# Batch 0's squared norms by TensorE from the turned operands, omega by ScalarE's queue, ScalarE's table loaded first

## The chip, the cores and the metric

The kernel runs on one core of a Trainium2 chip. The metric is the device time of one execution in microseconds (us). The kernel before takes 980.41 us as the median of three runs (978.39 to 980.9). Engine names are those of the profile: PE is TensorE, DVE is VectorE, ACT is ScalarE, POOL is GpSimd, SP is the engine whose queue issues the transfers.

## The reference

A linear attention over random features, and behind it two feed-forward layers on 2304 rows of 512 columns. Cut to what matters here:

```
scale = 1 / sqrt(sqrt(64))                    # q, k: 4 batches, 8 heads, 576 rows, 64 columns
phi(x):  proj = x @ omega.T                   # omega: 128 features x 64
         h    = proj - sum(x*x) / 2           # the squared norm of each row
         return exp(h - max(h)) / sqrt(128)
kv  = phi(k*scale).T @ v;  z = sum of phi(k*scale) over rows
out = phi(q*scale) @ kv / (phi(q*scale) @ z + 1e-6)
x   = relu(out @ w_in)**2 @ w_out             # layer 1: 512 -> 2048 -> 512
xn  = x / rms(x) * rms_g
out = (silu(xn @ w_gate) * (xn @ w_val)) @ w_out2
```

All in float32. The kernel splits each operand of the large products into a high and a low part and adds three products.

## The kernel before, in words

The program has no loop at run time. A planner (class Plan, L43 to L244) is given every piece of work as a node with an engine, a planned duration, a priority and the buffers that it reads and writes; it plays the pieces through once when the program is built, and the order in which it starts them is the order in which they stand in each engine's queue. Each queue is worked off in that order on the chip: an instruction whose input is late holds up all behind it on its engine. Buffers come from classes with a fixed number of slots (L301 to L307): "t", "h" and "acc" are the eight PSUM banks (2, 2 and 4), "ld" (3) holds row-wise loads, "lt", "tt" and "tr" (2, 4, 1) the turned ones, "st" (3) the raw weights, "dw" (2) the decoded ones, "sm" (24) small statistics.

Where the planner finds TensorE idle before its time 45 us it puts in a filler: two products of a matrix of ones into a spare bank, L480, whose result nobody reads (L478 to L483, L221).

Attention (L519 to L752) runs per batch over four pairs of heads and over the "remainder", the last 64 rows of all heads. For each pair, k and then q is loaded twice: turned (64 columns of two heads on the 128 partitions, 512 rows along them; `operand`, L534) as TensorE's stationary operand, and row-wise (L563). From the row-wise copy `row_norms` (L527) takes the squared norms: a square by POOL, ACT or DVE, whichever the planner finds free (L498 to L500), and a sum over each row by DVE (L531). `features` (L568) multiplies the turned operand by omega (L577) into two banks, takes each row's maximum on DVE (L586), combines it with the norm in two small instructions (L590), and exponentiates on ACT (L598). Products with v (L637, L640), transposes (L691, L740) and the products of q with kv (L697) follow.

Layer 1 of batch j (`moe1`, L766) follows the attention of batch j, while the attention of batch j+1 is interleaved. In batch 0 each of the 32 weight units is loaded (raw, 512 KB), decoded by ACT and DVE (`decode`, L419: L430, L433 or L435, L439, L441, L444), and split into high and low by a cast on ACT (L401) and a subtraction on DVE or POOL (L392). L812 and L842 are the two products of layer 1.

Omega's 64 rows are loaded twice, to both halves of the partitions, by SP's queue (L485, through the helper `dma`, whose transfers all have line L386), and scaled by ACT (L489), which is ACT's first instruction and so the one in front of which its function table is loaded.

Of the kernel before, what the change touches and what calls it, by code (L numbers as in the profile page):

```python
# [9 lines left out]
F32 = mybir.dt.float32  # L10
# [4 lines left out]
AF = mybir.ActivationFunctionType  # L15
ALU = mybir.AluOpType
# [231 lines left out]
def kernel(  # L248
# [23 lines left out]
    nc = tc.nc  # L272
    PSUM = bass.MemoryType.PSUM
    B, SR, H, _ = rest_v.shape
    _, HP, P, _, R, D = q_r.shape
# [10 lines left out]
    SCALE = float(D) ** -0.25  # L286
# [4 lines left out]
    const = ctx.enter_context(tc.tile_pool(name="const", bufs=1))  # L291
# [16 lines left out]
    plan = Plan(slots)  # L308
# [38 lines left out]
    ones = const.tile([P, P], F32R, name="ones")  # L347
    om2 = const.tile([P, M], F32, name="om2")
    oms = const.tile([P, M], F32, name="oms")
    g_sb = const.tile([P, KC], F32, name="g_sb")  # L350
    eps_sb = const.tile([P, 1], F32, name="eps_sb")
    v_t = [att.tile([P, 2, R, D + 1], F32, name=f"v{i}") for i in range(2)]
    vr_t = att.tile([P, H * (D + 1) + 8], F32, name="vr")[:, :H * (D + 1)].rearrange("p (h n) -> p h n", h=H)
    kv_t = [att.tile([P, 2, 80], F32, name=f"kv{i}")[:, :, :D + 1] for i in range(2)]
# [4 lines left out]
    b_oms = Buf(ap=oms)  # L359
# [7 lines left out]
    def f32(t):  # L367
        return t.bitcast(F32)
# [5 lines left out]
    def dve(n):  # L374
        return 0.07 + n * 0.00104

    def pool(n):
        return 0.19 + n * 0.00216
# [4 lines left out]
    def dma(prio, outap, inap, nbytes, r=(), w=(), after=()):  # L383
        return plan.add(
            "SP", nbytes / 311e3, prio,
            lambda: nc.sync.dma_start(out=outap(), in_=inap()), r, w, after, tail=2.0,  # L386
        )
# [73 lines left out]
    T0 = -40.0  # L461
# [10 lines left out]
    b_late, b_eps = Buf(ap=ones), Buf(ap=eps_sb)  # L472
    plan.add("DVE", 0.3, T0, emit_ones, w=[b_late])
    plan.add("POOL", 1.0, T0, lambda: make_identity(nc, ident), w=[b_const])
    plan.add("POOL", 0.3, T0 + 2, emit_late, w=[b_eps])
    b_vz = Buf(ap=vr_t)
    plan.add("POOL", 0.6, T0 + 1, emit_zero_rows, w=[b_vz])
    def filler(bank):  # L478
# [2 lines left out]
                             rhs=ones.rearrange("p (o n) -> p o n", o=1).to_broadcast([P, 2, P]), start=True, stop=True)  # L481

    plan.filler = Buf(["acc"]), filler  # L483
    b_om = Buf(ap=om2)
    for h in range(2):  # L485
        dma(T0, lambda h=h: om2[h * D:(h + 1) * D, :], lambda: omega_t, 32768, w=[(b_om, h)])
    dma(T0 + 30, lambda: g_sb, lambda: rms_g.rearrange("(k p) -> p k", p=P), 2048, w=[b_g])

    plan.add("ACT", 0.4, T0, lambda: nc.scalar.activation(out=oms, in_=om2, func=AF.Copy, scale=SCALE), [b_om], [b_oms])  # L489

    def copy(prio, out, src, n, rd, wr):

# [3 lines left out]
    def square(prio, x, xa, n):  # L496
        opts = (
            ("POOL", pool(n), lambda: nc.gpsimd.tensor_tensor(out=xa(), in0=xa(), in1=xa(), op=ALU.mult)),  # L498
            ("ACT", act(n), lambda: nc.scalar.activation(out=xa(), in_=xa(), func=AF.Square)),  # L499
            ("DVE", Shared(dve(n)), lambda: nc.vector.tensor_tensor(out=xa(), in0=xa(), in1=xa(), op=ALU.mult)),  # L500
        )
        plan.add(*opts[0][:2], prio, opts[0][2], [x], [x], alts=opts[1:])
# [16 lines left out]
    def attention(b):  # L519
        base = (b - 1) * float(C1) if b else -25.0  # L520
        step = 3.7 if b else 6.0
        lead = base - (6.0 if b else 2.85)
        long = b >= LONG
        rem_x, rem_p = [], []
        ssr = Buf(["sm"])

        def row_norms(prio, x, ss):  # L527
            square(prio, x, lambda: x.ap, 512)
            plan.add(
                "DVE", dve(512), prio,  # L530
                lambda: nc.vector.tensor_reduce(out=ss.ap[:, :8], in_=x.ap, op=ALU.add, axis=AX), [x], [ss],  # L531
            )

        def operand(ldp, src, cls):  # L534

            x = Buf(["lt", cls])
            dma(ldp, lambda: x.ap, src, 262144, w=[x])
            return x

        def rem_prep(pr0):  # L540
            rem_x[:] = [operand(lead, lambda: rest_t[b].rearrange("p h n -> p (h n)"), "tr")]
            xr = Buf(["ld"], view=lambda t: t.rearrange("p h r d -> p (h r) d"))
            dma(lead, lambda: xr.ap, lambda: rest_r[b], 262144, w=[xr])
            row_norms(pr0, xr, ssr)
            dma(lead, lambda: vr_t[P - SR:], lambda: rest_v[b], 133120, w=[b_vr])

        def pair(hp):
            banks = ["t"] if b else ["t", "h", "acc"] if hp < 3 else ["t", "acc"]
# [6 lines left out]
            ld = pb - 3.0  # L555
            dma(ld + 0.1, lambda: vt, lambda: v_r[b, hp], 266240, w=[bv])
            stats = {}

            def transposed(nm, p0):
                ss = stats[nm] = Buf(["sm"])  # L560
                src, src_t = (k_r, k_t) if nm == "k" else (q_r, q_t)
                xs = operand(ld, lambda: src_t[b, hp], "tt")
                x = Buf(["ld"], view=lambda t: t.rearrange("p h r d -> p (h r) d"))  # L563
                dma(ld + 0.05, lambda: x.ap, lambda: src[b, hp].rearrange("p h r d -> p (h r) d"), 262144, w=[x])
                row_norms(p0, x, ss)
                return xs
# [38 lines left out]
            u = step / 10.0  # L605
            pk, pq = Buf(["p"]), Buf(["p"])
            xk = transposed("k", pb)
            features(pb + u, pk, xk, ODD, stats["k"], list(last_q))
            if hp == 0:
                rem_prep(pb + u)  # L610
                rem_p[:] = [Buf(["pr"])]
                features(pb + 2 * u, rem_p[0], rem_x[0], ODD, ssr)
            pr = rem_p[0]
            xq = transposed("q", pb + 2 * u)
            last_q[:] = [features(pb + 4 * u, pq, xq, ODD, stats["q"])]

# [76 lines left out]
            def mm(h):  # L693
                np, qt = nps[h], qts[h]
                for r in range(R):
                    for cs in HALVES:
                        nc.tensor.matmul(np.ap[cs, r * D1:(r + 1) * D1],  # L697
                                         lhsT=qt.ap[:, r * P + cs.start:r * P + cs.stop],
                                         rhs=kvt[:, h, :], start=True, stop=True)
                if h == 0:  # L700
                    for g in range(2):
                        nc.tensor.matmul(np.ap[:SR, (R + g) * D1:(R + g + 1) * D1], lhsT=qrt.ap[:, g, :],
                                         rhs=kvt[:, g, :], start=True, stop=True)
# [477 lines left out]


    attention(0)
    for b in range(B):
        if b + 1 < B:
            attention(b + 1)
        moe1(b)
# [104 lines left out]
```

## Time and profile before

| | |
|---|---|
| median of three runs | 980.41 us (978.39 to 980.9) |
| the profiled execution, its own time | 981.26 us |
| its span, first to last instruction | 979.1 us |
| PE busy | 960.5 us (98%), 5996 instructions |
| DVE busy | 690.7 us (71%) |
| ACT busy | 513.9 us (52%) |
| POOL busy | 73.8 us (8%) |
| bytes moved | 179.46 MB, mean 183 GB/s |

A view of windows gives, for each stretch in us from the span's start, the busy time of each engine with the number of its instructions in brackets, the granted TensorE clock as a share of full speed, the busy share of the 16 DMA engines, and GB/s. A timeline row is start, duration, engine, line, operation, output and input, count, and in square brackets the idle time before it and what ended that. "PEld" is the load of TensorE's stationary operand, "SPq" a transfer being issued by SP. In the timeline a float32 product shows as two entries where the program's order has one row. The chain of waits is the work that ended last, followed back; a row of it is start, length, what.

### The profile page before, as it was taken

The page shows a single profiled execution, that of the slowest core. Times are in us where ns is not written, and L with a number is a line of the kernel's source. Part 1 is how long each engine was busy: PE and PEld are TensorE (multiplying, and loading weights), DVE is VectorE, ACT ScalarE, POOL GpSimd, SP SyncE. Part 2 cuts the span into 40 slices and gives each one's busy share as a digit, 9 for nine tenths or more (in the row PEclk, how much of TensorE's full clock was granted, in tenths as well). Part 3 has the DMA queues.
Part 4 walks back from the last instruction along what each step waited for, and adds up shares of the span by engine and source line. Part 5 has one row for each costly group of instructions (what it writes and reads, how often), then busy time and mean ns, then how long its engine had stood idle before and what let it go on. Part 6 is the DMA issues. An engine that isn't in the chain of part 4 may idle for free.

```text
span 979.1 us, 16214 instructions
## 1 busy us (share of the span) xinstructions
PE 960.5 (98%) x5996; PEld 794.5 (81%) x5996; DVE 690.7 (71%) x1363; ACT 513.9 (52%) x1075; POOL 73.8 (8%) x70
## 2 busy tenths in 40 slices
PE   8999989999999999999999999999999999999998
PEld 8877767787788787887889988888887888888886
DVE  6898977677655665554554988989797747567673
ACT  6887776665545544544555657654353443314220
POOL 1123012010000000000000210000000000000000
PEclk9999999999999999999999999999999999999999
DMA  8878788888777765588879454234233221212203
GB/s 264 278 221 276 229 270 287 294 287 282 243 229 255 236 205 200 173 273 289 302 263 334 130 149 128 79 113 129 83 119 123 75 84 33 76 46 74 68 29 108
DMA packets 74846, 179.46 MB, mean 183 GB/s; under 512 B 8848, under 2 KB 12048, under 8 KB 74768
## 3 DMA queue, kind: packets, MB, share of 16 engines
q1 hardware_dynamic: 74768, 178.43, 56.2%
q8 instruction: 47, 0.77, 0.3%
q14 instruction: 31, 0.25, 0.1%
HBM read 143.27 MB, written 35.13 MB: 182 GB/s over the span
## 4 chain that ended last, share of the span: by engine, by line
PE 84%; DVE 7%; DMA 5%; ACT 3%; issue 1%; SPq 0%; POOL 0%; DVEq 0%; ACTq 0%; POOLq 0%
PE h L812 18%; PE acc L842 17%; PE acc L1054 11%; PE t L1115 11%; PE h L1054 10%; PE t L1054 4%; PE t L577 3%; PE t L697 2%; PE t L637 1%; DVE cc L1074 1%; PE t L691 1%; PE acc L480 1%; PE h L1115 1%; DVE oa L1123 1%; DMA st<-in_w_out_dram 1%
## 5 line engine op out<-in xcount | busy, mean ns | idle before, releaser
L842 PE MATMUL acc<-g,wr 128*128 128x512 f32 (+1 forms) x660 | 154.4, 378 | 3.7 <-POOL g L392 2.1
L842 PEld LDWEIGHTS acc<-g,wr 128*128 128x128 f32 x660 | 114.4, 191 | 27.3 <-POOL g L392 2.7
L812 PE MATMUL h<-x,wr 128*128 128x512 f32 x528 | 135.0, 398 | 0.5 <-ACT wr L401 0.5
L401 ACT CAST wq<-wq 128x512 fp32r<-128x512 f32 x108 | 66.0, 618 | 103.8 <-PE t L1115 16.6
L1115 PE MATMUL t<-wq,ub 128*128 128x512 f32 x474 | 116.6, 391 | 1.4 <-DVE oa L1123 1.3
L812 PEld LDWEIGHTS h<-x,wr 128*128 128x128 f32 x528 | 97.3, 189 | 22.1 <-ACT wr L401 0.7
L1054 PE MATMUL acc<-x,wq 128*128 128x512 f32 x324 | 107.0, 389 | 0.1
L1115 PEld LDWEIGHTS t<-wq,ub 128*128 128x128 f32 x474 | 88.5, 188 | 22.0 <-DVE oa L1123 2.9
L392 DVE TENSOR_TENSOR wq<-wq 128x512 fp32r<-128x512 f32 x108 | 80.1, 750 | 32.5 <-ACT wq L401 32.0
L826 ACT ACTIVATE f<-h 128x512 f32<-128x512 f32 (+1 forms) x80 | 44.8, 559 | 91.0 <-PE h L812 90.9
L1054 PE MATMUL h<-x,wq 128*128 128x512 f32 x252 | 85.3, 390 | 0.0
L392 DVE TENSOR_TENSOR g<-f,g 128x512 fp32r<-128x512 f32 (+1 forms) x64 | 43.3, 677 | 48.8 <-ACT f L499 36.8
L1054 PEld LDWEIGHTS acc<-x,wq 128*128 128x128 f32 x324 | 60.8, 188 | 13.2 <-DVE cc L1074 0.6
L598 ACT ACTIVATE p<-t,sm 128x128 f32<-128x128 f32 x224 | 62.2, 383 | 16.4 <-DVE sm L590 16.1
L1054 PE MATMUL acc<-xa,wq 128*128 128x512 f32 x192 | 69.9, 389 | 0.0
L842 PE MATMUL acc<-g,wu 128*128 128x512 f32 (+1 forms) x300 | 68.2, 373 | 0.0
L439 ACT ACTIVATE dw<-st 128x512 f32<-128x512 f32 x68 | 46.6, 688 | 41.0 <-DMA st<-in_w_out_dram 11.8
L1074 DVE TENSOR_TENSOR cc<-acc,cc 128x512 f32<-128x512 f32 x84 | 57.7, 687 | 12.9 <-PE acc L1054 11.7
L1123 DVE TENSOR_TENSOR oa<-t,oa 128x512 f32<-128x512 f32 x75 | 50.8, 686 | 21.8 <-PE t L1115 21.3
L812 PE MATMUL h<-x,wu 128*128 128x512 f32 x240 | 61.8, 402 | 3.0 <-ACT wu L401 3.0
L586 DVE TENSOR_REDUCE sm<-t 128x4 f32<-128x512 f32 x62 | 40.8, 684 | 28.3 <-PE t L577 26.7
L1054 PE MATMUL h<-xa,wq 128*128 128x512 f32 x168 | 60.5, 389 | 0.0
(232 smaller groups left out, 1647.9 us busy)
## 6 DMA issues: line engine op xcount, KB each, us to landing
wr<-w1d SPq DMA_DIRECT2D x88, 512.0 KB, 4.5
st<-in_w_out_dram SPq DMA_DIRECT2D x28, 512.0 KB, 4.7
w1d<-wr SPq DMA_DIRECT2D x22, 512.0 KB, 3.9
st<-in_w_in_dram SPq DMA_DIRECT2D x16, 512.0 KB, 4.6
st<-in_w_gate_dram SPq DMA_DIRECT2D x12, 512.0 KB, 6.0
st<-in_w_val_dram SPq DMA_DIRECT2D x12, 512.0 KB, 5.5
st<-y SPq DMA_DIRECT2D x23, 256.0 KB, 4.0
v<-in_v_r_dram SPq DMA_DIRECT2D x16, 260.0 KB, 3.5
```

What stands on the lines that cost most here:

```text
L392: return lambda: en.tensor_tensor(out=lo(), in0=src(), in1=f32(hi()), op=ALU.subtract)
L401: first = plan.add("ACT", act(n), prio, lambda: nc.scalar.copy(out=hi(), in_=src()), rd, [whi], after, pre=[blo] if blo is not bhi else [])
L439: lambda: nc.scalar.activation(out=out(), in_=hf(), func=AF.Abs, scale=65536.0), [(st, 1)], [w])
L586: nc.vector.tensor_reduce(out=mx.ap[:, :R], in_=fp.ap, op=ALU.max, axis=AX)
L598: nc.scalar.activation(out=pbuf.ap[:, j, :], in_=fp.ap[:, i, :], func=AF.Exp, bias=mx.ap[:, i:i + 1])
L812: nc.tensor.matmul(hb.ap[:, :n], lhsT=u.ap[:, wl, kk * P:(kk + 1) * P], rhs=xcols(j, xl, kk)(), start=(gi == 0 and ii == 0), stop=(gi == l ...
L826: lambda: nc.scalar.activation(out=rb.ap[:, :n], in_=hb.ap[:, :n], func=AF.Relu), [hb], [rb])
L842: nc.tensor.matmul(accs[e].ap[:, :n], lhsT=u.ap[:, w, es], rhs=x.ap[:, :n], start=(c == 0 and i == 0), stop=(c == C1 - 1 and i == 2))
L1054: nc.tensor.matmul(bank.ap[:, cols], lhsT=u.ap[:, wl, c0 + kk * P:c0 + (kk + 1) * P], rhs=x[kk][xl].ap[:, :cols.stop - cols.start], start= ...
L1074: lambda: nc.vector.tensor_tensor(out=out.ap, in0=bank.ap, in1=x.ap, op=ALU.add), [bank, x], [out])
L1115: nc.tensor.matmul(o.ap, lhsT=x[xl].ap[:, c0:c0 + P], rhs=us[f"o{i}"].ap[:, wl, :], start=i == n == 0, stop=i == 1 and n == 2)
L1123: lambda: nc.vector.tensor_tensor(out=oa.ap, in0=o.ap, in1=oa.ap, op=ALU.add), [o, oa], [oa])
```

## The change

Four things are altered. In batch 0 the row-wise loads of q, k and the remainder (nine transfers of 256 KB) are dropped with their row norms; in their place `turned_norms` squares the turned operand on POOL, and TensorE multiplies each of its four 128-column pieces by a 128 x 2 matrix of zeros and ones ("heads"), which sums the squares of each head. The norms then lie in a PSUM bank, where the two small DVE instructions read them. Omega's two transfers are issued by ACT's queue instead of SP's; omega is scaled by DVE instead of ACT; and ACT's first activation is an exponential of one element of the ones, so that its table is loaded there. Batches 1 to 3 keep the row-wise norms.

```diff
+    warm = const.tile([P, 1], F32, name="warm")
+    heads = const.tile([P, 2], F32, name="heads")
...
+    def emit_heads():
+        nc.gpsimd.memset(heads, 0.0)
+        for h in range(2):
+            nc.gpsimd.memset(heads[h * D:(h + 1) * D, h:h + 1], 1.0)
+
+    b_heads = Buf(ap=heads)
+    plan.add("POOL", 0.4, T0 + 0.5, emit_heads, w=[b_heads])
...
-    b_om = Buf(ap=om2)
-    for h in range(2):
-        dma(T0, lambda h=h: om2[h * D:(h + 1) * D, :], lambda: omega_t, 32768, w=[(b_om, h)])
+    b_om, b_warm = Buf(ap=om2), Buf(ap=warm)
+    plan.add("ACT", 0.1, T0, lambda: nc.scalar.dma_start(
+        out=om2[:D], in_=omega_t), w=[(b_om, 0)], tail=2.0)
+    plan.add("ACT", 0.6, T0 + 0.1, lambda: nc.scalar.dma_start(
+        out=om2[D:], in_=omega_t), w=[(b_om, 1)], tail=2.0)
+    plan.add("ACT", 1.4, T0 + 0.2, lambda: nc.scalar.activation(out=warm, in_=f32(ones[:, :1]), func=AF.Exp), [b_late], [b_warm])
...
-    plan.add("ACT", 0.4, T0, lambda: nc.scalar.activation(out=oms, in_=om2, func=AF.Copy, scale=SCALE), [b_om], [b_oms])
+    plan.add("DVE", 0.2, T0, lambda: nc.vector.tensor_scalar(out=oms, in0=om2, scalar1=SCALE, scalar2=None, op0=ALU.mult),
+             [b_om], [b_oms])
...
+        def turned_norms(p0, x, banks):
+            x2 = Buf(["ld"], view=lambda t: t.rearrange("p h r d -> p (h r d)"))
+            plan.add("POOL", pool(512), p0,
+                     lambda: nc.gpsimd.tensor_tensor(out=x2.ap, in0=x.ap, in1=x.ap, op=ALU.mult), [x], [x2])
+            ss = Buf(banks)
+
+            def mm():
+                for i in range(R):
+                    nc.tensor.matmul(ss.ap[:, 2 * i:2 * i + 2], lhsT=x2.ap[:, i * P:(i + 1) * P], rhs=heads,
+                                     start=True, stop=True)
+
+            plan.add("PE", 0.22 * R, p0, mm, [x2, b_heads], [ss])
+            return ss
+
...
         def rem_prep(pr0):
+            nonlocal ssr
             rem_x[:] = [operand(lead, lambda: rest_t[b].rearrange("p h n -> p (h n)"), "tr")]
-            xr = Buf(["ld"], view=lambda t: t.rearrange("p h r d -> p (h r) d"))
-            dma(lead, lambda: xr.ap, lambda: rest_r[b], 262144, w=[xr])
-            row_norms(pr0, xr, ssr)
+            if b:
+                xr = Buf(["ld"], view=lambda t: t.rearrange("p h r d -> p (h r) d"))
+                dma(lead, lambda: xr.ap, lambda: rest_r[b], 262144, w=[xr])
+                row_norms(pr0, xr, ssr)
+            else:
+                ssr = turned_norms(pr0, rem_x[0], ["t", "h", "acc"])
...
             def transposed(nm, p0):
-                ss = stats[nm] = Buf(["sm"])
                 src, src_t = (k_r, k_t) if nm == "k" else (q_r, q_t)
                 xs = operand(ld, lambda: src_t[b, hp], "tt")
+                if not b:
+                    stats[nm] = turned_norms(p0, xs, banks)
+                    return xs
+                ss = stats[nm] = Buf(["sm"])
```

The planner lays all queues out anew. TensorE at the program's start, before: "ones" are the fillers, "oms" the scaled omega, lt the turned k and then q of pair 0, tr the remainder, and after that lt the k of pair 1.

```order
L480 MATMUL acc_180<-ones 128x256 x12
L577 MATMUL t_211<-oms,lt_188 128x128
...
L577 MATMUL h_230<-oms,lt_193 128x128
...
L577 MATMUL acc_257<-oms,tr_223 128x128
...
L480 MATMUL acc_180<-ones 128x256 x4
L577 MATMUL t_289<-oms,lt_245 128x128
...
L480 MATMUL acc_180<-ones 128x256 x28
L577 MATMUL t_365<-oms,tt_249 128x128
```

TensorE at the same place now (the ld tiles hold the squares; lt_189 and lt_195 are k and q of pair 0, tt_232 is k of pair 1):

```order
L489 MATMUL acc_182<-ones 128x256 x14
L611 MATMUL t_221<-oms,lt_189 128x128
...
L555 MATMUL h_241<-heads,ld_216 128x2 x4
L555 MATMUL h_254<-heads,ld_239 128x2 x4
L611 MATMUL acc_265<-oms,tr_211 128x128
...
L555 MATMUL h_287<-heads,ld_234 128x2 x4
L489 MATMUL acc_182<-ones 128x256 x2
L611 MATMUL t_304<-oms,lt_195 128x128
...
L555 MATMUL t_319<-heads,ld_259 128x2 x4
L489 MATMUL acc_182<-ones 128x256 x8
L611 MATMUL h_354<-oms,tt_232 128x128
```

The remainder now comes ahead of pair 0's q, a norm of four products stands beside each operand (nine in all), and fillers fall from 90 to 36 in the whole program.

ScalarE at its start, before (p holds the exponentials of a pair, pr those of the remainder, and an L499 row is a square for a norm):

```order
L489 ACT_TABLE_LOAD
L489 ACTIVATE oms<-om_76 128x128
L499 ACTIVATE ld_200<-ld_200 128x512
L499 ACTIVATE ld_207<-ld_207 128x512
L598 ACTIVATE p_213<-t_211,sm_243 128x128 x4
L499 ACTIVATE ld_226<-ld_226 128x512
L598 ACTIVATE p_213<-t_212,sm_247 128x128 x4
L499 ACTIVATE ld_272<-ld_272 128x512
L499 ACTIVATE ld_276<-ld_276 128x512
L598 ACTIVATE pr_259<-acc_257,sm_300 128x128 x4
L598 ACTIVATE pr_259<-acc_258,sm_309 128x128 x4
L598 ACTIVATE p_232<-h_230,sm_274 128x128 x4
```

ScalarE at its start now (ld_276 is the remainder of batch 1, row-wise):

```order
L494 DMA om_76<-in_omega_t_dram 64x128
L496 DMA om_76<-in_omega_t_dram 64x128
L498 ACT_TABLE_LOAD
L498 ACTIVATE warm<-ones 128x1
L632 ACTIVATE p_223<-t_221,sm_246 128x128 x4
L632 ACTIVATE p_223<-t_222,sm_250 128x128 x4
L512 ACTIVATE ld_276<-ld_276 128x512
L632 ACTIVATE pr_267<-acc_265,sm_292 128x128 x4
L632 ACTIVATE pr_267<-acc_266,sm_294 128x128 x4
L441 ACTIVATE dw_368<-st_285 128x512
L632 ACTIVATE p_306<-t_304,sm_329 128x128 x4
L632 ACTIVATE p_306<-acc_305,sm_339 128x128 x4
```

Batch 0's squares are gone from ScalarE; one square of batch 1 stands in front of the remainder's exponentials, and the first step of decoding a weight (L441, which was L439) has moved up to just behind them.

## Rows read from the trace of the kernel before

**Rows 1.** Windows: busy PE, PEld, DVE, ACT, POOL (count); clock; DMA share; GB/s.

```profile
5.00:50.00 45.00, 44.56 (x612) 39.81 (x613) 38.18 (x126) 37.40 (x113) 5.16 (x5) 1.00 0.88 285
50.00:170.00 120.00, 113.09 (x811) 86.56 (x811) 102.43 (x236) 89.42 (x195) 25.43 (x19) 0.96 0.79 256
170.00:979.00 809.00, 799.92 (x4571) 665.53 (x4566) 549.94 (x1003) 385.66 (x767) 42.03 (x38) 1.00 0.52 167
```

**Rows 2.** Chain of waits, 0 to 80 us: start, length, what.

```profile
1.36 2.14 DMA om<-in_omega_t_dram
3.57 1.28 ACT L489
7.38 3.99 DMA lt<-in_k_t_dram
12.66 3.54 PE acc L480 x28
31.26 1.09 PE t L577 x16
```

**Rows 3.** What TensorE waited for, 50 to 170 us: total, times, longest.

```profile
PE h L812 <- ACT wu L401: 3.0, 1, 3.0
```

**Rows 4.** Windows of TensorE alone: busy PE (count), clock, DMA share, GB/s.

```profile
52.00:54.00 2.00, 0.84 (x10) 1.00 0.98 303
54.00:58.00 4.00, 4.00 (x20) 0.57 0.68 206
122.00:126.00 4.00, 0.99 (x5) 1.00 0.95 328
126.00:130.00 4.00, 4.00 (x13) 0.57 0.75 246
156.00:160.00 4.00, 2.47 (x21) 1.00 0.69 231
160.00:164.00 4.00, 4.00 (x44) 0.57 0.50 148
```

**Rows 5.** Timeline, 0 to 46 us, several engines.

```profile
0.73 1.21 SPq L386 DMA_DIRECT2D om<-in_omega_t_dram  x2
1.05 2.93 PE L480 MATMUL acc<-ones 128*128 128x256 f32 x12 [1.05 <-DVE ones L464]
...
5.23 2.08 PE L577 MATMUL t<-oms,lt 64*128 64x128 f32 x16 [1.25 <-ACT oms L489]
...
12.76 0.63 ACT L499 ACTIVATE ld<-ld 128x512 f32<-128x512 f32 x1 [0.80 <-DMA ld<-in_k_r_dram]
...
14.40 2.15 ACT L598 ACTIVATE pr<-acc,sm 128x128 f32<-128x128 f32 x8
...
41.19 0.59 ACT L401 CAST x<-t 128x512 fp32r<-128x512 f32 x1 [1.62 <-PE t L740]
41.67 2.18 ACT L598 ACTIVATE p<-acc,sm 128x128 f32<-128x128 f32 x8
```

**Rows 6.** Groups by line and form, TensorE, 5 to 48 us: the fillers.

```profile
L480 PE MATMUL acc<-ones 128*128 128x256 f32 x78 | 12.0, 294 | 0.0
```

**Rows 7.** Timeline of TensorE, 30 to 65 us: stationary operands of 128 and 64 columns.

```profile
32.83 0.60 PE L691 MATMUL h<-ident,p 128*128 128x128 f32 x4
...
41.08 0.69 PE L637 MATMUL t<-v,p 128*64 128x65 f32 x16
```

**Rows 8.** One line each: durations in ns (min/median/max), first and last start.

```profile
L531 DVE TENSOR_REDUCE sm<-ld x36: 654/679/689, 7.0 to 244.5; 128x8 f32<-128x512 f32 x36
L498 POOL TENSOR_TENSOR ld<-ld x10: 1038/1040/1287, 17.2 to 218.4; 128x512 f32<-128x512 f32 x10
L590 DVE SCALAR_TENSOR_TENSOR sm<-sm,sm x144: 123/155/1021, 8.8 to 400.0; 128x4 f32<-128x4 f32 x144
```

**Rows 9.** Timeline of POOL, 32 to 34.7 us.

```profile
32.63 2.04 POOL L498 TENSOR_TENSOR ld<-ld 128x512 f32<-128x512 f32 x2 [4.14 <-DMA ld<-in_k_r_dram]
```

**Rows 10.** Timeline of DVE beside it.

```profile
33.31 0.39 DVE L590 SCALAR_TENSOR_TENSOR sm<-sm,sm 128x4 f32<-128x4 f32 x1
```

## Prediction

> **What bounds the kernel now.** I read the windows first, then the chain of waits, TensorE's waits, and the timeline of the first 50 us. TensorE is busy 799.92 of the 809 us behind 170 us [rows 1]: whatever is won or lost before that goes through to the end almost whole, since the later work hangs on TensorE. Ahead of that lie two stages with different limits.
>
> From 5 to 50 us, batch 0's attention, TensorE counts as busy 44.56 of 45 us, but 78 of its products there are fillers [rows 1, 6]. In the chain of waits 28 of them last 3.54 us [rows 2], so one costs 0.126 us and the 78 some 9.8 us. DVE and ACT are busy 38.18 and 37.40 us there: TensorE, DVE and ACT all run close to full, and none can move far ahead alone.
>
> From 50 to 170 us, layer 1 of batch 0 with the attention of batch 1, TensorE is idle 120 - 113.09 = 6.9 us, while DVE and ACT (102.43 and 89.42 us) decode and split the weights [rows 1]. The idle time lies in three stalls, and behind each of them stand 4 us in which the granted clock is 0.57 [rows 4], that is mostly the lower level of 1.2 GHz; each of these costs 4 x 0.43 = 1.7 us more. Stage loss: 6.9 + 3 x 1.7 = 12.1 us. The longest stall is 3.0 us for a weight's cast on ACT [rows 3].
>
> **The change, part by part.** *Start.* Before, the chain is omega's transfer (2.14 us from the second issue at 1.36), the table load (1.28) and the scaling on ACT; the first product of omega stands at 5.23 [rows 2, 5]. Now the table load lies beside the transfer. If ACT issues omega at the same times and it lands as fast, it is there at 3.5, and DVE's scaling, not shown before, lies between one small DVE instruction (0.155 us) [rows 8] and the 1.28 us of the table load that it must stay below to save anything; I take 0.25, so 3.8. SP's queue loses the 1.21 us of omega's issues [rows 5], so the turned k is issued at 0.73 instead of 1.94 at the earliest; before it was there by 5.23, within 3.3 us of its issue, so now by 4.0. Both are covered: 14 fillers instead of 12 at 2.93 / 12 = 0.244 us run to 1.05 + 3.42 = 4.47. The start moves by -0.76 us. Were omega as slow from ACT as the 3.99 us of a large transfer [rows 2], it would be 5.6 instead: +0.4.
>
> At the same moment POOL squares k. While POOL worked from 32.63 to 34.67, a DVE instruction of 0.155 us begun at 33.31 took 0.39 and ended as POOL's first square did [rows 8 to 10]. So if POOL is first, the scaling ends near 3.5 + 1.04 + 0.25 = 4.8, and the start moves by -0.4.
>
> The Trainium skill says of this ("SBUF — State Buffer", Who interferes with whom) that DVE and GpSimd share a pair of ports which the first holds for its whole instruction, and that a tensor_scalar can need it. The trace's 0.39 beside 0.155 agrees; by the rule the nine squares moved to POOL also hold up DVE, though the two small DVE instructions now read the norm from PSUM and no longer two SBUF inputs, so by it they go free.
>
> *Fillers.* 22 behind the first block instead of 78: 56 x 0.126 = -7.1 us of TensorE.
>
> *Norms.* Nine times four products, two entries each. No row shows a product with two columns. By 64-column stationary operands (16 entries in 0.69, 0.043 each) a norm costs 0.34 us; by the 128-column transposes (4 in 0.60, 0.15 each) 1.2 [rows 7]; by omega's products, float32 in two entries (16 in 1.09, 0.068) [rows 2], 0.55. The last are nearest in kind; I take 9 x 0.55 = +4.9 us, between +3.1 and +10.8. So TensorE alone would be ahead by 0.76 + 7.1 - 4.9 = 3.0 us.
>
> *POOL and the banks.* Nine squares of 1.04 us [rows 8] lie on an engine busy 5.16 of 45 us. The first norm is ready at about 4.0 + 1.04, under the sixteen entries of k's features (4.47 to 6.55 at the 2.08 us of before). The remainder's norm waits for POOL's third square, about 7.2, some 0.1 us. Each norm holds one of the eight banks until its four small DVE instructions have run; I cost that at nothing, because fillers stand where TensorE would wait; where the cover is missing it is the slower rival below.
>
> *ACT.* It loses batch 0's squares and the scaling, but now one square of batch 1 stands ahead of the remainder's exponentials, and its row-wise load is the twelfth transfer of SP's queue. Before, the eleventh large load landed at 12.76 [rows 5]; with 1.25 us less in front and 0.25 MB more at 285 GB/s (0.9), the new one lands near 12.4, its square (0.63) ends at 13.0, and the remainder's exponentials start there instead of at 14.40: -1.4 us. From there to the last exponentials of batch 0 ACT's order has the same 64 exponentials, and two decode steps, two weight casts and two squares more, one copy of a turned tile fewer: +5 x 0.63 = +3.2. Before it took 14.40 to 43.85, 1.62 us of it in one wait for TensorE [rows 5]. Without that wait now 13.0 + 27.8 + 3.2 = 44.0. So batch 0's attention ends no earlier (+0.1), though TensorE alone could do 3.0; but ACT then is 3.2 us of later work ahead.
>
> *DVE and transfers.* Nine sums of 0.679 us [rows 8] and one square leave DVE, about 6.8 us; nine loads of 256 KB (2.36 MB, 8.3 us at 285 GB/s) leave the queue. Both were covered; they come back as weights that are decoded earlier.
>
> *Layer 1.* ACT's lead of 3.1 us (3.2 - 0.1) is a little above the longest of the three stalls. Bounds: all three go with their slow clock (-12.1), or none, or another as long as the worst appears (+4.7). Because every queue is laid out anew, I credit one stall only, the 3.0 us for a cast with its 1.7 us: -4.7.
>
> *Sum.* +0.1 - 4.7 = -4.6 us against the profiled execution's 981.26, 2.2 of which lie outside the span: 976.7. The median of the runs lies 0.85 below that execution, so 975.8.
>
> **The rivals.** *A, the forecast*, 975.8, its own range 972 to 978.5.
>
> *B, the transfers and norms were hidden anyway.* ACT's lead is eaten where DVE is busy 102 of 120 us, stalls of the same sum remain, and only the start's 0.76 us come through: 980.4 - 0.8 = 979.6. For it: the three engines are near full in both stages, and squares of batch 1 have moved to ACT. Against: 6.8 us really leave DVE.
>
> *C, TensorE is the bound throughout.* The 3.0 us come whole, and two stalls go: the longest (4.7) and one of 1.5 + 1.7: 980.4 - 3.0 - 7.9 = 969.5. For it: the chain of the first 50 us is nearly all TensorE. Against: the ACT count above.
>
> *D, slower: the fillers that went kept TensorE's clock up.* A norm that is quicker than it was planned leaves TensorE waiting in the attention of batch 0 where no filler stands, since the order is fixed. Each gap of 1.2 us or more has cost itself and 1.7 us of half clock [rows 4], 2.9 in all. It decides from two such gaps on: 5.8 - 0.8, and the stalls of layer 1 stay: 985.4. For it: 56 fillers fewer. Against: from 5 to 50 us before, 0.44 us idle in all.
>
> *E, the change doesn't do what it says at its head:* omega from ACT's queue lands late, and the start, at 5.6, is 1.2 us later than forecast; otherwise as A: 977.0.
>
> **How the numbers follow.** A 0.45, B 0.26, C 0.14, D 0.10, E 0.05. About 0.3%, 2.9 us, is what a measurement of this kernel can tell from no change: the bounds are 977.5 and 983.3. Faster: 0.8 of A (0.36), C (0.14), more than half of E (0.03), 0.53. Within: the rest of A (0.09) and E (0.02), B (0.26), 0.37. Slower: D, 0.10. The range reaches from C's end to between B and D, 970 to 982.
>
> **What would show it.** In the changed profile: the first omega product at 4.4 to 4.9; a norm's eight entries in 0.4 to 0.7 us; the last exponentials of batch 0 ending within a microsecond of 44.0, with two more weights decoded by then; TensorE idle from 50 to 170 us down from 6.9 to some 4 us, and one stretch of half clock fewer. I am wrong if norms cost 1 us or more, if the granted clock falls before 45 us, or if the stalls of layer 1 sum to 12 us again.

## The result, and the profile after

The changed kernel takes 986.5 us (median of 8 runs, 983.49 to 991.87) where the kernel before took 980.34 beside it: a ratio of 1.008, 95% interval 1.006 to 1.010. It is 6 to 8 us slower; forecast were 4.6 us less. The profiled execution after took 990.53 us with a span of 988.6, at the upper end of its runs, so its rows are read for what happened and where, and the sizes are taken from the medians.

The windows of before [rows 1], now:

```profile
5.00:50.00 45.00, 42.62 (x488) 38.78 (x488) 26.71 (x89) 27.29 (x85) 9.28 (x10) 0.77 0.64 202
50.00:170.00 120.00, 115.06 (x911) 89.64 (x908) 105.96 (x258) 93.66 (x215) 24.06 (x18) 0.97 0.77 251
170.00:988.00 818.00, 811.65 (x4607) 668.06 (x4606) 549.70 (x1008) 389.82 (x773) 41.61 (x38) 1.00 0.51 167
```

Two things are to be seen. In the first stage TensorE still counts as busy 42.62 of 45 us, but it got through 488 instructions in place of 612, at a mean granted clock of 0.77 in place of 1.00 (before, the clock's record begins only at 9.99 us, and sixteen entries of omega's products took 2.08 us at 5.23 [rows 5] against 1.09 later [rows 2], so its 1.00 hides a half-speed start); DVE and ACT, busy 38.18 and 37.40 us before, fell to 26.71 and 27.29, by more than the work taken off them: they wait for TensorE. And the last stage, which the change doesn't touch, is longer, with TensorE's idle time still small (6.4 us now, 9.1 before). 4.2 us of the 9 more are lateness brought in from ahead, as the course of the work below shows; the rest is lost in the stage itself.

The head of the program answers to [rows 5]; timeline, several engines:

```profile
0.74 0.55 ACTq L494 DMA_DIRECT2D om<-in_omega_t_dram  x1
1.32 0.61 ACTq L496 DMA_DIRECT2D om<-in_omega_t_dram  x1
1.96 1.28 ACT L498 ACT_TABLE_LOAD   x1 [1.96 <-issue]
3.74 2.04 POOL L550 TENSOR_TENSOR ld<-lt 128x512 f32<-128x512 f32 x2 [1.50 <-DMA lt<-in_k_t_dram]
4.98 0.88 DVE L501 TENSOR_SCALAR oms<-om 128x128 f32<-128x128 f32 x1 [3.98 <-DMA om<-in_omega_t_dram]
5.92 1.16 PE L611 MATMUL t<-oms,lt 64*128 64x128 f32 x16 [1.50 <-DVE oms L501]
7.01 1.26 PE L555 MATMUL h<-heads,ld 128*128 128x2 f32 x8
8.50 1.87 PE L555 MATMUL h<-heads,ld 128*128 128x2 f32 x8 [0.23 <-POOL ld L550]
```

The table load lies beside the transfer, as forecast. But omega lands 3.66 us behind its second issue (4.98 - 1.32), not 2.14 as from SP's queue [rows 2], and its scaling lasts until POOL's second square is done: 4.98 + 0.88 = 5.86, against 3.74 + 2.04 = 5.78. The Trainium skill states ("SBUF — State Buffer", Who interferes with whom) that the two share a pair of ports which one holds for its whole instruction; the trace agrees, with 0.88 us where the prediction took 0.25. With omega alone, where POOL runs nothing beside it, the same instruction takes 0.23:

```profile
4.58 0.23 DVE L493 TENSOR_SCALAR oms<-om 128x128 f32<-128x128 f32 x1 [3.58 <-DMA om<-in_omega_t_dram]
```

The first product of omega stands at 5.92, not at 4.47, and 0.69 later than before.

Below 45 us, the windows of TensorE alone (busy, count, granted clock, DMA share, GB/s):

```profile
5.00:10.00 5.00, 3.85 (x31) 0.77 0.99 322
10.00:15.00 5.00, 5.00 (x30) 0.50 0.84 255
15.00:20.00 5.00, 5.00 (x31) 0.50 0.50 138
20.00:25.00 5.00, 5.00 (x61) 0.52 0.36 148
```

From 7.70 to 24.76 us TensorE was granted 1.2 GHz, though between 7 and 25 us it was never idle for more than 0.23 us. What it did before the clock fell: 1.50 us of idle time up to 5.92, sixteen entries of omega, and a norm begun at 7.01. A norm's eight entries last 1.87 us at half speed; the first norm behind it shows what they last at 2.4 GHz:

```profile
25.10 1.05 PE L555 MATMUL acc<-heads,ld 128*128 128x2 f32 x8
```

The last exponentials of batch 0 end at 55.99 + 1.19 = 57.2, where 44.0 was forecast:

```profile
55.99 1.19 ACT L632 ACTIVATE p<-acc,sm 128x128 f32<-128x128 f32 x4
```

The places of the stalls of layer 1 [rows 4] are full, without idle time and with the clock at 2.4 GHz:

```profile
122.00:126.00 4.00, 4.00 (x29) 1.00 0.67 242
126.00:130.00 4.00, 4.00 (x44) 1.00 0.88 290
156.00:160.00 4.00, 4.00 (x35) 1.00 0.89 321
160.00:164.00 4.00, 4.00 (x45) 1.00 0.94 326
```

One more difference has no answer in the change's text: in layer 2, where both kernels issue the same products in the same kind of rows, twelve of them in a row last 2.96 us now and 2.88 before. Its rows stand at the experiment that explains it.

### The profile page after: what moved, and what is told of

Same layout as the page of the kernel before. It is cut to its first block, busy times and chain, and to the rows that moved or that the text cites. A ratio compares the mean times of both kernels' runs of the same rounds, so it can differ in the third digit from the quotient of the medians.

```text
span 988.6 us, 16233 instructions
## 1 busy us (share of the span) xinstructions
PE 972.7 (98%) x6014; PEld 799.6 (81%) x6014; DVE 682.5 (69%) x1354; ACT 512.3 (52%) x1072; POOL 77.7 (8%) x77
## 4 chain that ended last, share of the span: by engine, by line
PE 88%; DVE 5%; DMA 4%; ACT 1%; issue 1%; POOL 1%; SPq 0%; POOLq 0%; ACTq 0%; DVEq 0%
PE h L846 18%; PE acc L876 18%; PE acc L1088 13%; PE t L1149 12%; PE h L1088 11%; PE t L1088 3%; PE t L611 3%; PE h L1149 2%; PE t L731 1%; PE t L671 1%; DMA ld<-in_k_r_dram 1%; PE t L725 1%; DMA ld<-in_rest_r_dram 1%; DMA st<-in_w_in_dram 1%; DMA tr<-in_rest_t_dram 1%
## 5 line engine op out<-in xcount | busy, mean ns | idle before, releaser
L876 PE MATMUL acc<-g,wr 128*128 128x512 f32 (+1 forms) x660 | 151.8, 374 | 2.0 <-POOL g L394 1.2
L1149 PE MATMUL t<-wq,ub 128*128 128x512 f32 x474 | 119.6, 396 | 0.5 <-DVE oa L1157 0.3
L394 DVE TENSOR_TENSOR wq<-wq 128x512 fp32r<-128x512 f32 x108 | 79.1, 740 | 35.1 <-ACT wq L403 34.7
L394 DVE TENSOR_TENSOR g<-f,g 128x512 fp32r<-128x512 f32 (+1 forms) x67 | 46.2, 690 | 49.1 <-ACT f L512 39.1
L632 ACT ACTIVATE p<-t,sm 128x128 f32<-128x128 f32 x216 | 59.5, 381 | 27.6 <-DVE sm L624 27.6
L441 ACT ACTIVATE dw<-st 128x512 f32<-128x512 f32 x68 | 46.6, 686 | 39.2 <-DMA st<-in_w_out_dram 8.5
```

What stands on the lines that cost most here:

```text
L394: return lambda: en.tensor_tensor(out=lo(), in0=src(), in1=f32(hi()), op=ALU.subtract)
L441: lambda: nc.scalar.activation(out=out(), in_=hf(), func=AF.Abs, scale=65536.0), [(st, 1)], [w])
L632: nc.scalar.activation(out=pbuf.ap[:, j, :], in_=fp.ap[:, i, :], func=AF.Exp, bias=mx.ap[:, i:i + 1])
L876: nc.tensor.matmul(accs[e].ap[:, :n], lhsT=u.ap[:, w, es], rhs=x.ap[:, :n], start=(c == 0 and i == 0), stop=(c == C1 - 1 and i == 2))
L1149: nc.tensor.matmul(o.ap, lhsT=x[xl].ap[:, c0:c0 + P], rhs=us[f"o{i}"].ap[:, wl, :], start=i == n == 0, stop=i == 1 and n == 2)
```

## The experiments

Theories: **T1**, the clock: TensorE works at half speed over the norm products of two columns. **T2**, the head: omega late, its scaling held up. **T3**, batch 1's row-wise loads, on which ACT and POOL wait in order. Later came **T4** (the norm products are costly in themselves), **T5** against **T6** (where the tiles lie, against the new order or the chip, slows layer 2) and **T7** against **T8** (distance of two operands, against the place of one).

### Wider norm products, nothing else

```diff
-    heads = const.tile([P, 2], F32, name="heads")
+    heads = const.tile([P, P], F32, name="heads")
...
-  nc.tensor.matmul(ss.ap[:, 2 * i:2 * i + 2], lhsT=x2.ap[:, i * P:(i + 1) * P], rhs=heads,
+  nc.tensor.matmul(ss.ap[:, i * P:(i + 1) * P], lhsT=x2.ap[:, i * P:(i + 1) * P], rhs=heads,
...
```

> Order, buffers and queues are those of the changed kernel; only the moving operand of each of the 72 norm products of batch 0 is 128 columns wide in place of 2 (the other 126 columns are zeros, their sums are not read). T1 (TensorE runs nearly idle through the stretches of two-column products, its granted clock stands at half from 7.7 to 24.8 us, and batch 0's attention is done at half speed): the clock is at full for most of 5 to 25 us, batch 0's work is 6 to 9 us less late, the kernel ends at 977 to 981 us. T2 (omega's late landing and its 0.88 us scaling set the clock back) and T3 (batch 1's row-wise loads arrive late): nothing of theirs is changed, 986 us, or a little more for the wider products.

979.73 us (ratio 1.0018, 1.0007 to 1.003). The clock stays at full from 4.77 to 55.97 us. The same windows as above:

```profile
5.00:10.00 5.00, 4.35 (x48) 1.00 0.99 325
10.00:15.00 5.00, 5.00 (x54) 1.00 0.92 317
15.00:20.00 5.00, 4.85 (x82) 1.00 0.89 306
20.00:25.00 5.00, 5.00 (x99) 1.00 0.23 66
```

and a norm of 128 columns lasts 1.05 to 1.16 us, little longer than one of two at full clock (0.95 to 1.05):

```profile
10.06 1.16 PE L555 MATMUL h<-heads,ld 128*128 128x128 f32 x8
```

T1 holds, and T2 and T3, whose causes were left in place, fall as the main one. An idle stretch stands ahead of omega here too (1.23 us, beside 1.50) and the clock did not fall behind it. The width costs little: at full clock the products last nearly as long with 2, 32 and 128 columns (1.05, 1.08 and 1.16 us for eight entries).

### The two halves of the change apart

Omega by SP's queue and scaled on ACT in the changed order; the norms alone, planned anew; omega and the table alone, planned anew.

```diff
-    plan.add("ACT", 0.1, T0, lambda: nc.scalar.dma_start(
+    plan.add("ACT", 0.1, T0, lambda: nc.sync.dma_start(
...
```

> The changed kernel with omega loaded by SyncE's queue and scaled on ScalarE again; the norms stay on TensorE, the order of everything else stays. T2: the first omega product comes at about 5.2 us in place of 5.9, TensorE has no idle stretch before it, the clock stays at full after 7.7 us, and the time is 978 to 981 us. T1: the first omega product comes earlier too, but the clock still falls before 10 us and stays at half for 15 us or more; 985 to 987 us. T3: 985 to 987 us as well.

> The kernel before with one part of the change, planned anew: batch 0's norms by TensorE from turned operands; omega is loaded and scaled as before. T1: a half-speed stretch of 10 us or more before 30 us, 984 to 987 us. T2: no such stretch, 977 to 981 us. T3: 984 to 987 us, with the granted clock at full from 10 to 40 us and the loss at the waits for batch 1's loads.

> The kernel before with the other part of the change, planned anew: omega by ScalarE's queue and scaled on VectorE, the table loaded first; batch 0's norms stay row-wise with their loads, fillers and VectorE's sums. T1: omega's first product within 0.7 us of the kernel before's 5.23, no half-speed stretch of 10 us before 40 us, 979 to 982 us. T2: the first product near 5.9, the clock falls before 10 us, 984 us or more. T3: 979 to 982 us.

986.24, 985.43 and 977.83 us (1.0071, 1.0071, 0.9991; the last interval 0.9979 to 1.0003). Omega back on SP and off DVE brings its first product to 5.42 us, the clock stands at half from 8.26 to 25.33, and the time is that of the changed kernel: T2 is not the main loss. (It isn't a clean test of the gaps: a wait of 1.77 us for POOL's square opens at 7.57.) The norms alone run at half speed until 20.04 us. I read from this that the norms were the whole loss and omega worth nothing. That was wrong in size, for a reason that all these kernels share and that shows only behind 500 us.

### The kernel before again, and with thin fillers

```diff
-            nc.tensor.matmul(bank[:, :2 * P].rearrange("p (o n) -> p o n", o=2), lhsT=ones,
-                             rhs=ones.rearrange("p (o n) -> p o n", o=1).to_broadcast([P, 2, P]), start=True, stop=True)
+            nc.tensor.matmul(bank[:, :2], lhsT=ones, rhs=ones[:, :2], start=True, stop=True)
```

> The kernel before, unchanged, as a control on the chip that runs the others: 978 to 980 us. What is asked of its trace: whether the stalls of layer 1 (at 122 and 157 us in the first trace) and the full pace of the products after 550 us (0.227 us apart) belong to this kernel or to one run. If they belong to the kernel, both stand there again, and what the changed kernel wins back of its late start between 120 and 170 us is the missing stalls; if to the run, the stalls are elsewhere or gone and the products after 550 us are 0.231 to 0.233 us apart as in the traces of the other kernels of this study, and the tail of the changed kernel (5 us lost after 550) is no effect of the change.

> The kernel before with its own order and its row-wise norms; each of the 78 fillers moves 2 columns in place of 256. T1 (products that move few columns leave the clock at half): the granted clock stands at half for 10 us or more before 30 us, batch 0's attention is 5 to 12 us late, 982 to 986 us. The rival T4 (the norm products are costly in themselves, by their weight loads or their place in the chain from POOL's squares, and the clock follows from the gaps): nothing of that is in this kernel, the clock rises at about 9 us as before, 977 to 980 us.

The control took 978.96 us (1.0004), the thin fillers 985.2 (1.0062, 1.0039 to 1.0085). Without any norm product and in the order of before, the clock stood at half from 12.07 to 25.72 us, in the control from 12.26 to 15.67. The windows, control first:

```profile
10.00:15.00 5.00, 4.04 (x36) 0.73 0.91 291
15.00:20.00 5.00, 5.00 (x48) 0.93 0.63 153
20.00:25.00 5.00, 5.00 (x88) 1.00 0.91 291
```

```profile
10.00:15.00 5.00, 4.19 (x39) 0.71 0.96 309
15.00:20.00 5.00, 5.00 (x25) 0.50 0.80 228
20.00:25.00 5.00, 5.00 (x61) 0.50 0.23 88
```

TensorE is as busy in both, and in both idle time lies ahead of the fall or around it (1.23 and 0.72 us with thin fillers, 2.04 in the control), so the fall itself may be due to that; what the fillers decide is how soon the clock is back. So the fillers of before did a second work for the clock. T4 falls as the main cause. The control's trace also has the stalls of layer 1 again, some 2 us later, so they belong to the order of before; and its products of layer 2 keep their pace, as do those of the kernel with thin fillers, while those of the changed kernel and of every kernel that has its new tiles don't.

### 32 columns, and a first attempt at a better kernel

> The changed kernel with its order kept and 32 moving columns in each norm product, between the 2 of the change and the 128 that gave 979.73 us. T1: the loss shrinks with the columns moved; the half-speed stretch of 7.7 to 24.8 us is shorter but not gone, 981 to 985 us. T4 (width matters only when the product is as long as its weight load takes): the eight entries still take 0.95 us or more, the clock falls as with 2 columns, 986 us.

> A version that may beat both: norms by 128-column products, their cost in the order's table set to the 1.0 us per eight that they took (1.76 in the changed kernel), omega by SyncE's queue first in its order and scaled on VectorE, the table still loaded first. T1: full clock from about 5 us to 40 us, no stall of TensorE over 2 us before 40 us, 976 to 979 us, the kernel before or a little under it. If the rest of the loss is in the row-wise loads of batch 1 (T3), it stays at 979 to 981 us.

986.96 and 989.39 us: both off. With 32 columns the clock's record has no entry before 23.05 us, but a norm lasts 1.91 us as at half clock, and nothing is won over two columns. That is the time that T4 had for it, not T1's; but its layer 2 is slower too (0.2334 us from product to product, against 0.2321 in the changed kernel, some 2 us in all), so the run by itself doesn't tell the two apart. The second keeps its clock from 4.77 to 144.72 us as expected and is slower all the same: it is stalled elsewhere (TensorE 26.85 of 30 us busy from 140 to 170), and its layer 2 is slow, which neither T1 nor T3 has a place for.

### Where the tiles lie

The change puts two new tiles, warm and heads, into the pool "const". With their rounding they move everything behind them on that side of the memory by 64 bytes a partition: x, xb, ub and g, which are one operand of layer 2's products, from 41152 to 41216 and so on in the compiled program. The other operand, wq, lies in a pool of the other side and stays at 171968. Layer 1 takes both operands (x or g with wr or wu) from the moved side. The wide norms moved it by 544 bytes, omega alone by 32, 32 columns by 160.

```diff
     eps_sb = const.tile([P, 1], F32, name="eps_sb")
+    const.tile([P, 16], F32, name="pad")
```

> The kernel before, its order untouched, with one unused tile of 64 bytes a partition behind eps_sb, so that every tile that follows in the pools on that side (x, xb, ub, g, xq among them) lies 64 bytes higher, as the two new tiles of the change (warm and heads) put it; the tiles of the other side (wq, xa) stay. T5 (the products after 550 us, whose two operands lie on the two sides, run slower by where the tiles lie): 0.2267 us from product to product becomes 0.231 to 0.234 after 550 us, nothing before 500 us changes, and the time is 984 to 986 us, 5 to 7 us over the kernel before. Rival T6 (the new order itself, or the chip's state, slows the late products): 978 to 980 us and 0.2267 us as before.

> The changed kernel with an unused tile that makes the sum of the new tiles 2048 bytes a partition in place of 64. T5: the late products are 0.2267 us apart again, the half-speed stretch of 7.7 to 24.8 us stays, 979 to 982 us. T6: 986 us.

> Norm products of 128 columns (which gave 979.73 us) and the same filling up to 2048 bytes. T1 and T5 together: no half-speed stretch before 40 us, late products 0.2267 us apart, 972 to 975 us, faster than both kernels. T6: 979.7 us.

> Omega by ScalarE's queue alone, row-wise norms (which gave 977.83 us), filled up to 2048 bytes. T5: late products 0.2267 us apart, 971 to 974 us; the part of the change that concerns omega and the table is then worth 5 us or more, hidden until now by the late products. T6: 977.8 us.

Measured: the kernel before with 64 unused bytes 986.4 us (1.0075, 1.0053 to 1.0098); the changed kernel filled up to 2048 bytes 978.74 (1.0003, 0.999 to 1.0017); wide norms filled up 972.21 (0.9946, 0.9927 to 0.9966); omega alone filled up 970.44 (0.9924, 0.9906 to 0.9943). T5 holds in all four, and T6 falls. The same row of twelve products, of the control, of the changed kernel, of before with 64 bytes, and of the changed kernel filled up:

```profile
659.49 2.88 PE L1115 MATMUL t<-wq,ub 128*128 128x512 f32 x12
```

```profile
663.14 2.96 PE L1149 MATMUL t<-wq,ub 128*128 128x512 f32 x12
```

```profile
659.43 2.96 PE L1116 MATMUL t<-wq,ub 128*128 128x512 f32 x12
```

```profile
652.77 2.88 PE L1150 MATMUL t<-wq,ub 128*128 128x512 f32 x12
```

From start to start that is (2.88 - 0.389) / 11 = 0.2265 us and (2.96 - 0.394) / 11 = 0.2333. Over all some 1640 products of 512 columns of layer 2 the mean is 0.2270 in the control and 0.2321 in the changed kernel: 1640 x 0.0051 = 8.4 us, which is what 64 unused bytes cost in the medians (8.5; by the ratio 7.3). The granted clock is 1.00 in both. Layer 1's products of 512 columns follow each other every 0.2282 us in both, and it keeps its count in equal time: 350 to 420 us, control and changed kernel:

```profile
350.00:420.00 70.00, 70.00 (x556) 1.00 0.55 194
```

```profile
350.00:420.00 70.00, 70.00 (x556) 1.00 0.56 193
```

### Distance or place, and the period

```diff
-    edge.tile([P, 8], F32, name="edge")
+    edge.tile([P, 24], F32, name="edge")
```

> The kernel before with its unused edge tile 96 bytes in place of 32, which puts wq, xa and the attention's tiles 64 bytes lower and leaves x, xb, ub, g where they were. T7: the distance changes by 64 bytes, 0.231 to 0.234 us after 550 us, 984 to 987 us. T8 (the place of x, ub and g alone decides): 0.2267 us, 978 to 980 us.

> Both sides moved: wq and xa 64 bytes lower, x, xb, ub and g 448 bytes higher, so that their distance changes by 512 bytes. T7: 0.2267 us after 550 us, 978 to 980 us. T8: 0.231 to 0.234 us, 984 to 987 us.

> The kernel before with 512 unused bytes in place of 64. T7 (what counts is how far apart the two operands lie, modulo 512 bytes): 0.2267 us from product to product after 550 us, as in the kernel before. If a multiple of 2048 is needed: 0.231 to 0.234.

> The kernel before with 256 unused bytes. T7: 0.231 to 0.234 us after 550 us, some 6 us more in all. If 256 bytes were the period: 0.2267 us.

> The kernel before with 128 unused bytes, between the 64 that slow the late products and the 256 that do not. Period of 128 bytes: 0.2267 us from product to product after 550 us, 976 to 980 us. Period of 256 bytes: 0.231 to 0.234 us, 984 to 987 us.

One execution each: 987.44, 980.55, 977.72, 975.94 and 982.49 us. The pace of the same row tells more than these times; moved on the other side alone, and on both:

```profile
660.46 2.96 PE L1115 MATMUL t<-wq,ub 128*128 128x512 f32 x12
```

```profile
658.41 2.88 PE L1116 MATMUL t<-wq,ub 128*128 128x512 f32 x12
```

With 512 and 256 bytes it is 2.88, with 128 bytes 2.94; the last two:

```profile
654.61 2.88 PE L1116 MATMUL t<-wq,ub 128*128 128x512 f32 x12
```

```profile
655.49 2.94 PE L1116 MATMUL t<-wq,ub 128*128 128x512 f32 x12
```

T8 falls, since moving wq's side alone is enough and moving both undoes it. T7 holds, but not with the 512 bytes that it had named: 32, 64, 128, 160 and 544 bytes are slow, 256, 512 and 2048 are not, as a period of 256 bytes would have it. What counts is the distance between the two sides. One thing doesn't fit the distance between a product's own operands: products of xa and wq, which lie on one side and keep theirs, are slow as well (0.233 us on average in the changed kernel, 0.227 before). They stand among products of x, so a product's neighbours may matter too; that was argued, not tried. The kernel before has an unused tile of 32 bytes at the other side's edge, which happens to set that distance right. What waits for what in the slow case was not tried.

## Why the prediction was wrong

The parts, by the ratios to the kernel before (978 us in the runs of the four filled-up kernels):

| step | us | from |
|---|---|---|
| omega, table and the new order, tiles in place | -7.4 | omega alone, filled up, 0.9924 |
| norms by TensorE, 128 columns | +2.1 | wide norms, filled up, 0.9946 |
| two columns instead of 128: the clock | +5.6 | the changed kernel filled up, 1.0003 |
| tiles moved by 64 bytes | +7.5 | the changed kernel, 1.008 |
| sum | +7.8 | |

Each ratio has an interval of about 2 us to either side, so the +2.1, a difference of two of them whose intervals overlap, is the least certain; the 1.008 comes from runs on another occasion, with its own runs of before.

The profiles give the same course, one execution each. Below, how much later than in the first profile of before TensorE has done the same work, in us, by the starts of its useful products weighted by their length:

| at (time of before) | changed | filled up | wide, filled up | omega, filled up | before with 64 bytes |
|---|---|---|---|---|---|
| 46 | +11.2 | +6.8 | +2.8 | +1.4 | +3.3 |
| 105 | +12.5 | +5.7 | +1.6 | +0.8 | +3.1 |
| 166 | +4.2 | -3.2 | -7.3 | -8.8 | +1.4 |
| 445 | +4.2 | -3.9 | -7.9 | -8.6 | +0.7 |
| end | +9.6 | -5.4 | -9.0 | -10.6 | +5.9 |

The control, the kernel before in another execution, stands in the same table at +2.5, +3.1, +2.8, +2.0 and +0.5, so 3 us between two profiles mean nothing by themselves; the half-speed loss is in the first row, the stalls that went between the second and third, the place of the tiles between the last two.

- **The step that failed: "whatever is won or lost before that goes through to the end almost whole", taken to mean that nothing else happens there.** The sum has no term behind 170 us, because no instruction there was changed. The passing on itself held (filled up: -3.2 at 166 us, -5.4 at the end). What changed is where the late products' tiles lie: +7.5 us. Nothing in the profile of before could give the size, but the diff shows two new tiles in the first pool of the program, ahead of nearly all others, and the kernel has an unused tile at its edge; I read past both.
- **Fillers and norms (-7.1, +4.9).** The fillers did go, and the first sign is right as a count of work. The norms were priced by omega's products, 0.55 us; at full clock they took 0.95 to 1.05, near the upper row (the transposes, 1.2), so 9 x 0.45 = 4 us more. But the larger error is that the sum knew one clock for both: +5.6 us. The prediction had sixteen entries of omega's products at 2.08 us [rows 5] and sixteen at 1.09 [rows 2] and did not ask why they differ by nearly two. This is rival D, which had 0.10: its premise (the fillers kept the clock up) was right. Its mechanism, two gaps of 1.2 us or more that each cost themselves and a short half-speed stretch, was not: there is one such gap, 1.50 us before 5.92, the wide norms have nearly the same one and kept their clock, and the half-speed stretch lasts 17 us without a gap over 0.23. D's price of 5.8 beside the 5.6 of the runs, and its 985.4 beside 986.5, are luck.
- **The start (-0.76).** +0.69: both bad cases named in the prediction, the slow landing and POOL's lock on DVE, came together (5.92, not 4.47). With omega back on SP's queue and scaled on ACT the time is the same (986.24 beside 986.5).
- **ACT (last exponentials at 44.0).** 57.2: TensorE was the bound at half speed, and the start of the remainder's exponentials did not move (14.41 for 14.40). At full clock, with 128 columns, they end at 47.3 (49.3 filled up), still 3 us and more behind the forecast.
- **Layer 1 (one stall, -4.7).** Too small: in the table the changed kernel wins back 8.3 us between 105 and 166. Both stalls behind 120 us and their half-speed rows are gone. They are gone with omega alone as well, where the nine loads and sums are still there, so it is the new order that removes them and not the work taken off DVE and the queue; what in the order does it was not isolated. The half-speed row behind the second stall is not in every execution of the old order either (not in before with 64 bytes), so its 1.7 us is no fixed price; and the idle time of [rows 4] adds up to 5.7 of the 6.9 us, the three stalls are not all of it. Windows of omega alone, filled up, and of the control:

```profile
120.00:140.00 20.00, 20.00 (x134) 1.00 0.88 315
155.00:170.00 15.00, 15.00 (x100) 1.00 0.95 325
```

```profile
120.00:140.00 20.00, 17.16 (x144) 0.91 0.87 274
155.00:170.00 15.00, 13.20 (x108) 0.89 0.72 250
```

Without the two terms that I did not have, the wide norms filled up come to 972.21 us, just inside the forecast's own range of 972 to 978.5. That is partly luck: by the table it was 1.6 us late at 105, where +0.1 was forecast, and won 8.9 by 166, where 4.7 was credited. Of the three signs that I named for being wrong two came (norms of 1 us and more, the clock below 45 us); the third did not.

The best version is omega by ACT's queue with the row-wise norms and the tiles in place: 970.44 us, 7.4 us under the kernel before. So the part of the change that looked like nothing is the one to keep, and the norms by TensorE showed no gain in any form tried here (+2.1 us at best, barely clear of noise).

## What to carry to other kernels

Work that TensorE does for nobody may keep its clock up: when such fillers are replaced, look at the granted clock of what replaces them, not at the time they took. A new tile, however small, moves every tile behind it; before a change is judged, see from an untouched late stage of the trace whether the same products still follow each other at the same pace, and fill the new tiles up so that the rest stays where it was. Test both halves of a change only when such a side effect is out of the way, else each half carries it and hides its own worth.

## What the runs showed of the hardware that was not expected

- 64 bytes more between the two operands' tiles made TensorE's 128x512 products 3.0% slower in the rows above (0.2265 to 0.2333 us) and 2.2% over all of layer 2 (0.2270 to 0.2321), at a granted clock of 1.00; shifts of 256, 512 and 2048 bytes were not slower.
- A float32 norm product lasted nearly as long with 128 moving columns (1.05 to 1.16 us for eight entries) as with two (0.95 to 1.05), both at full clock.
- The granted clock can stand at half while TensorE counts as busy: 5.00 of 5.00 us at 0.50 from 10 to 15 us in the changed kernel. Where the record has not begun, the view reads 1.00 all the same (32 columns: first entry at 23.05 us, norms at 1.91 us before).
- DVE's scaling of omega took 0.23 us with POOL idle, and 0.88 and 0.49 us (changed kernel, wide norms) beside POOL's squares, ending 0.08 us behind them both times.
- Omega took 3.66 us from its second issue by ACT's queue in the changed kernel and 3.27 with omega alone (first product at 4.86 us); by SP's queue 2.14 before and 3.06 in the changed order. So the queue alone does not set it.
